# Attention ahead of an MLP on one core: the matmuls of two pairs of heads grouped by kind

## The chip, the cores and the metric

The kernel runs on one core of a Trainium2 chip. The metric is the device time of one execution in microseconds: the median of the runs of one kernel on one chip. Runs of this kernel agree within about 0.3%.

## The reference

The program computes a sigmoid attention for 8 batches, 12 heads, 448 positions and a head size of 64, and feeds its result, 3584 tokens of 768 values, to a two-layer MLP (768 to 2048 to 768).

```python
scores = q @ k.T / sqrt(64) - log(448)          # per batch and head
attn = 1 / (1 + exp(-scores))
x = (attn @ v), heads side by side               # 3584 x 768
h = x @ w_in
out = (h / (1 + exp(-1.702 * h))) @ w_out        # 3584 x 768
```

The MLP weights arrive as float64 and are turned into float32 on the core. This document is about the attention; the MLP (796.5 us of the span, from 262.5 us on) is the same in both kernels.

## The kernel before

**Work.** A *pair* is two heads of one batch, which fill the 128 partitions; there are 48 pairs. A *unit* is two pairs, 2u and 2u+1; there are 24. The 448 keys of a head are cut into three chunks of 128 (`NC`) and 64 that are left over.

- `scores(n, c)` (matmuls at L577) makes the scores of one chunk of one pair: three terms by two heads, 6 matmuls, into two PSUM banks. q and k come as a rounded part and a rest, which `split_pair` makes with a cast (ACT, L442, or DVE, L443) and a subtraction (DVE, L448).
- `scores_left(n)` (L593) makes the left-over scores of both pairs of a unit at once, in the four 64x64 quarters of the array, from the unsplit `qkraw`.
- `sigmoid` (ACT, L563) reads the two banks of one such step and writes an `a` tile in SBUF; those of the left-over scores have a ring `al` of one.
- `values(n, c)` (L608) multiplies one chunk of `a` with v, into the two banks of the unit's `av`: one bank for each pair. `values_left` (L621) adds the left-over keys of both pairs and closes both banks.
- `to_x` copies the result out of PSUM (ACT, L658, or DVE, L660). x is kept by blocks of 512 tokens, and a batch has 448, so a pair's 448 columns fall into one or two blocks: one copy for each part, into `x32` tiles of 128 x 512 that several pairs of different batches fill. When a block of a pair is full, one DMA (`split_x`) writes it to `xd` in DRAM.

**Banks.** Scores, left-over scores and `av` all take their banks from four places of two banks each, q0 to q3, in turn (`two_banks`); a place is free for the next user when the sigmoid, or the copies, that read it are done.

**Order.** `Plan` lists tasks and emits each engine's instructions in one fixed order. PE takes units of work from two streams, the attention first; inside a unit it is the order of the list. A task that has `alone = False` is not looked at when the planner decides whether a unit can begin. ACT, DVE and SP take, by estimated times, the task with the smallest key of those that are ready; `plan.early` raises a task to just before another. On the chip each engine works through its own list in order, and waits on semaphores.

**Beside the attention** run the loads of q, k (`qkraw`), v (`vraw`) and of the float64 weights (`w`, 1536 KB each), and 16 decodes of weights. A decode has a sign on ACT (L487), one exponent step on ACT or DVE (L494 or L495), and six more operations on DVE (the longest at L504 and L506). All DMAs are issued by SP in one order. After the attention the MLP begins with `first_block` (matmuls into `h`, L800); its first bank is the one that the last `av` had.

Of the kernel before, what the change touches and what calls it, by code (L numbers as in the profile page):

```python
# [8 lines left out]
F32 = mybir.dt.float32  # L9
# [10 lines left out]
P = 128  # L20
T = 512
# [15 lines left out]

# [42 lines left out]
class Plan:  # L80
# [244 lines left out]
def sigmoid_attention_mlp(ctx: ExitStack, tc: tile.TileContext, qk, v, w, out):  # L325
    nc = tc.nc
# [3 lines left out]
    NP = H // 2  # L330
# [183 lines left out]
    x32, wrote, xs = {}, {}, {}  # L514
# [121 lines left out]
    def x32_places(b, p):  # L636

        for block, into, cols in places(b):
            fresh = (block, p) not in x32
            if fresh:  # L640
                x32[block, p] = buffer("x32")
                wrote[block, p] = []
            xb = x32[block, p]

            def first(xb=xb, block=block):
                if xb.tile is None:
                    make(xb, "x32", [P, T], F32, f"x32_{block}_{p}")

            yield block, xb, first, into, cols

    copies = []

    def to_x(b, p, t, ps):
        bank = (b * NP + p) % 2
        for block, xb, first, into, cols in x32_places(b, p):
            n = cols.stop - cols.start
            copies.append(on_either(
                (0.2 + 0.00075 * n, lambda xb=xb, into=into, cols=cols: nc.scalar.copy(  # L658
                    xb.tile[:, into], ps.tile[:, bank, cols])),
                (0.15 + 0.00105 * n, lambda xb=xb, into=into, cols=cols: nc.vector.tensor_copy(  # L660
                    xb.tile[:, into], ps.tile[:, bank, cols])),
                [t], [xb, ps], first,
            ))
            wrote[block, p].append(copies[-1])
        split_x(b, p)

    def split_x(b, p):

        if b:
            xb = x32[b - 1, p]  # L670
            spilled[b - 1, p] = dma(lambda: spill[b - 1][p // NJ][:, p % NJ], lambda: xb.tile, P * T * 4 / 1024,
                                    wrote[b - 1, p], [xb])

    def make_x(block, k):
        x = buffer("pair")
        n = NJ * T

        def first():
            if x.tile is None:
                make(x, "pair", [P, 2, 4, T], F32R, f"x{block}_{k}")  # L680

        t = [dma(lambda j=j: x.tile[:, 1, j].bitcast(F32), lambda j=j: spill[block][k][:, j], P * T * 4 / 1024,
                 [spilled[block, k * NJ + j]], [x], first) for j in range(NJ)]
# [8 lines left out]
    def attention():  # L692

        units, late, held_ = [], [], 0  # L700
        for n, (b, p) in enumerate(pairs):
            t_q, qkr, t_v, vr = load_pair(b, p)
            t_s, s = split_pair(b, p, t_q, qkr)
            firsts.append(t_s)
            left = scores_left(n, [first, (t_q, qkr)], held_ + 1) if n % 2 else None
            chunks = [scores(n, c, [t_s] if n else t_q[: c + 1], s, held_ + 1 + n % 2 + c) for c in range(NC)]
            run = [t for t, _, _ in chunks]
            if n % 2 == 0:
                first, chunks0, pair0 = (t_q, qkr), chunks, (b, p)
            else:  # L710

                units.append([left[0]])
                held_ += 1
                ps = two_banks(held_)
                both = [
                    [values(m, c, got[1], got[2], t_v, vr, ps) for c, got in enumerate(cs)]
                    for m, cs in ((n - 1, chunks0), (n, chunks))
                ]
                both[1].append(values_left(*left[1:], t_v, vr, ps))
                late.append(both[0])  # L720
                copied = len(copies)
                for pair in (pair0, (b, p)):
                    to_x(*pair, both[1][-1], ps)
                urgent.append(copies[copied:])
            if n > 2 and n % 2:

                plan.early += [(t, run[0]) for t in urgent[n // 2 - 1]]

            with_v = late.pop(0) if late else []
            for t in run[2:] + with_v:  # L730
# [220 lines left out]
    def triple(one, blocks_before):  # L951
# [5 lines left out]
        def x_leaf(v):  # L957
            k, n = divmod(v, 3)
            b = plan.slot()
            view = held(b, f"x{one}_{v}", XB)  # L960
            t = dma(lambda: view().rearrange("p (j t) -> p j t", j=NJ), lambda: spill[one + n][k], P * XB * 4 / 1024,
                    [spilled[one + n, k * NJ + j] for j in range(NJ)], [b])
# [340 lines left out]
```

## Time and profile before

| | |
|---|---|
| median of 3 runs (lowest, highest) | 1059.7 us (1059.66, 1063.46) |
| the profiled execution | 1060.78 us, span of its instructions 1059.0 us |
| PE busy, of the span | 1043.6 us, 99% |
| DVE busy | 843.4 us, 80% |
| ACT busy | 554.5 us, 52% |
| attention, to the first matmul of the MLP | 262.5 us |

The page gives busy times over the whole span. The attention and the MLP have different limits, so the prediction reads the attention by itself: the timeline (start, duration, engine, line, operation, and in brackets the idle time of the engine before it and what ended it), the chain of waits (the work that ended last, traced back; start, duration, what), and the waits of PE.

### The profile page before, as it was taken

The page shows a single profiled execution, that of the slowest core. Times are in us where ns is not written, and L with a number is a line of the kernel's source. Part 1 is how long each engine was busy: PE and PEld are TensorE (multiplying, and loading weights), DVE is VectorE, ACT ScalarE, POOL GpSimd, SP SyncE. Part 2 cuts the span into 40 slices and gives each one's busy share as a digit, 9 for nine tenths or more (in the row PEclk, how much of TensorE's full clock was granted, in tenths as well). Part 3 has the DMA queues.
Part 4 walks back from the last instruction along what each step waited for, and adds up shares of the span by engine and source line. Part 5 has one row for each costly group of instructions (what it writes and reads, how often), then busy time and mean ns, then how long its engine had stood idle before and what let it go on. Part 6 is the DMA issues. An engine that isn't in the chain of part 4 may idle for free.

```text
span 1059.0 us, 13676 instructions
## 1 busy us (share of the span) xinstructions
PE 1043.6 (99%) x5300; PEld 777.5 (73%) x5300; DVE 843.4 (80%) x770; ACT 554.5 (52%) x543; POOL 0.2 (0%) x4
## 2 busy tenths in 40 slices
PE   8999999999999999999999999999999999999997
PEld 4454545454788888888888788888888888788886
DVE  5988788873999856788898989999884596888684
ACT  7888788885655523434544444332443263534342
POOL 0000000000000000000000000000000000000000
PEclk9999999999999999999999999999999999999999
DMA  9899999883799997657656665869775545445765
GB/s 353 305 334 382 337 352 324 303 318 123 299 383 401 355 388 258 238 187 236 226 169 211 224 206 181 285 214 354 275 243 191 196 139 189 148 151 150 233 199 192
DMA packets 109104, 271.44 MB, mean 256 GB/s; under 512 B 8560, under 2 KB 69104, under 8 KB 106992
## 3 DMA queue, kind: packets, MB, share of 16 engines
q1 hardware_dynamic: 109040, 270.57, 73.1%
q8 instruction: 42, 0.69, 0.2%
q14 instruction: 22, 0.18, 0.1%
HBM read 185.60 MB, written 84.93 MB: 255 GB/s over the span
## 4 chain that ended last, share of the span: by engine, by line
PE 89%; DVE 4%; DMA 3%; ACT 2%; issue 1%; SPq 0%; ACTq 0%; DVEq 0%
PE p L800 54%; PE av L608 11%; PE sc L577 9%; PE h L800 6%; PE o_q L800 6%; PE av L621 2%; PE sc L593 2%; DMA qkraw<-qk 1%; DMA w<-c 1%; DMA w<-f 1%; DMA c<-wc 1%; DVE gp L1026 1%; ACT gp L1014 1%; DVE h L743 0%; ACT o L1156 0%
## 5 line engine op out<-in xcount | busy, mean ns | idle before, releaser
L800 PE MATMUL p<-gp,w 128*128 128x512 f32 x1440 | 329.5, 390 | 2.8 <-DVE gp L1026 1.2
L800 PE MATMUL p<-xp,w 128*128 128x512 f32 x1440 | 327.9, 389 | 1.0 <-DVE xp L1026 1.0
L800 PEld LDWEIGHTS p<-gp,w 128*128 128x128 f32 x1440 | 269.7, 188 | 61.3 <-DVE gp L1026 2.0
L800 PEld LDWEIGHTS p<-xp,w 128*128 128x128 f32 x1440 | 270.2, 188 | 57.5 <-DVE xp L1026 1.4
L563 ACT ACTIVATE a<-sc,bias 128x896 f32<-128x896 f32 x168 | 158.5, 1019 | 14.9 <-PE sc L577 10.9
L608 PE MATMUL av<-a,vraw 128*64 128x448 f32 x576 | 118.6, 547 | 0.0
L577 PEld LDWEIGHTS sc<-qk 64*128 64x128 f32 x846 | 75.8, 184 | 40.8 <-issue 14.0
L577 PE MATMUL sc<-qk 64*128 64x448 f32 x846 | 98.4, 373 | 2.6 <-DVE qk L448 2.0
L608 PEld LDWEIGHTS av<-a,vraw 128*64 128x64 f32 x576 | 37.1, 136 | 59.6 <-issue 56.4
L1026 DVE TENSOR_TENSOR gp<-h,gp 128x2048 fp32r<-128x2048 f32 x31 | 70.9, 2288 | 9.3 <-ACT gp L1014 8.9
L1156 ACT COPY h<-p 128x2048 f32<-128x2048 f32 x18 | 33.7, 1875 | 82.6 <-PE p L800 53.2
L800 PE MATMUL h<-x,w 128*128 128x512 f32 x288 | 66.6, 390 | 1.3 <-DVE x L660 1.3
L800 PE MATMUL o_q<-g,w 128*128 128x512 f32 x288 | 66.6, 389 | 1.2 <-ACT graw L856 1.2
L1190 DVE TENSOR_TENSOR h<-h,p 128x2048 f32<-128x2048 f32 x23 | 52.1, 2284 | 18.6 <-PE p L800 11.4
L1014 ACT CAST gp<-h 128x2048 fp32r<-128x2048 f32 x23 | 44.0, 1912 | 43.5 <-PE p L800 36.2
L800 PEld LDWEIGHTS h<-x,w 128*128 128x128 f32 x288 | 54.0, 188 | 13.3 <-DVE x L660 2.1
L800 PEld LDWEIGHTS o_q<-g,w 128*128 128x128 f32 x288 | 54.0, 188 | 12.8 <-ACT graw L856 1.6
L1156 ACT COPY o<-p 128x1536 f32<-128x1536 f32 x18 | 25.9, 1443 | 59.3 <-PE p L800 19.2
L448 DVE TENSOR_TENSOR qk<-qkraw,qk 128x896 fp32r<-128x896 f32 x47 | 51.2, 1089 | 6.4 <-ACT qk L442 5.9
L743 DVE TENSOR_TENSOR h<-h,h 128x2048 f32<-128x2048 f32 x24 | 54.7, 2285 | 0.1
L763 ACT CAST wc<-ws 128x384 fp32r<-128x384 f32 (+1 forms) x57 | 32.2, 580 | 42.2 <-DVE ws L743 26.8
L1014 ACT CAST xp<-x 128x1536 fp32r<-128x1536 f32 x19 | 28.1, 1480 | 39.4 <-PE p L800 32.3
(107 smaller groups left out, 975.0 us busy)
## 6 DMA issues: line engine op xcount, KB each, us to landing
w<-c SPq DMA_DIRECT2D x140, 384.0 KB, 4.4
w<-c SPq DMA_DIRECT2D x52, 768.0 KB, 4.6
w<-w SPq DMA_DIRECT2D x16, 1536.0 KB, 10.0
c<-wc SPq DMA_DIRECT2D x56, 384.0 KB, 5.4
qkraw<-qk SPq DMA_DIRECT2D x47, 448.0 KB, 6.5
vraw<-v SPq DMA_DIRECT2D x24, 448.0 KB, 4.9
xd<-x SPq DMA_DIRECT2D x42, 256.0 KB, 4.6
c<-wc SPq DMA_DIRECT2D x14, 768.0 KB, 7.2
```

The source lines that it names most:

```text
L448: lambda: nc.vector.tensor_tensor(lo(), src(), hi().bitcast(F32), op=ALU.subtract),
L563: nc.scalar.activation(a.tile, ps.tile[:, :, :S], AF.Sigmoid, bias=bias, scale=scale)
L577: nc.tensor.matmul(ps.tile[:, j, :S], lhsT=src[kk][rows, S + c * P : S + (c + 1) * P], rhs=src[qq][rows, :S], start=i == 0, stop=i == len( ...
L593: nc.tensor.matmul(ps.tile[cols, j, :S], lhsT=src.tile[rows, S + NC * P :], rhs=src.tile[rows, :S], start=True, stop=True, skip_group_chec ...
L608: nc.tensor.matmul(ps.tile[cols, n % 2, :S], lhsT=vr.tile[:, at : at + D], rhs=a.tile[:, j], start=c == 0, stop=False, skip_group_check=True,)
L743: return task("DVE", cost, lambda: nc.vector.tensor_tensor(out(), x(), y(), op=op), deps, uses)
L763: t_hi = on_either((act(n), lambda: nc.scalar.copy(into()[:, 0], node.view())), (cast(n), lambda: nc.vector.tensor_copy(into()[:, 0], node ...
L800: nc.tensor.matmul(ps, lhsT=ws[:, a, c * P : (c + 1) * P], rhs=x[:, d, k], start=start and i == 0 and j == 0, stop=stop and i == len(todo) ...
L1014: t_hi = on_either((act(n), lambda: nc.scalar.copy(part(0)(), node.view())), (cast(n), lambda: nc.vector.tensor_copy(part(0)(), node.view())),
L1026: nc.vector.tensor_tensor(part(1)(), node.view(), part(0)().bitcast(F32), op=ALU.subtract)
L1156: t = on_either((act(self.n), lambda: nc.scalar.copy(view(), node.view())), (dve(self.n), lambda: nc.vector.tensor_copy(view(), node.view())),
L1190: nc.vector.tensor_tensor(view(), x.view(), y.view(), op=ALU.add if s0 == s else ALU.subtract)
```

## The change

PE's list of one unit is now: scores of pair 2u, scores of pair 2u+1, left-over scores of both, products with v of both pairs, left-over products. Only the first step of a unit (`LEADERS`) decides whether it can begin. The eight steps of a unit take the four bank places twice round; before, places were counted so that a unit advanced by one place.

`to_x` copies both banks of `av` in one instruction (128 x 896, ACT or DVE) into an `x32` tile that belongs to the unit alone, and writes each part of it to `xd` with its own DMA: 64 to 448 columns of one or two pairs. There are three such tiles (eight of the smaller ones before), and seven `a` tiles (five before).

```diff
-    qk=2, vraw=3, a=5, al=1, raw64=2, e=4, qkraw=5, x32=8,
+    qk=2, vraw=3, a=7, al=1, raw64=2, e=4, qkraw=5, x32=3,
...
+LEADERS = 1
...
+    def to_x(b, p, t, ps):
+
+        xb = buffer("x32")
+
+        def rows():
+            make(xb, "x32", [P, 2, S], F32, f"x32_{b}_{p}")
+
+        c = on_either((0.97, lambda: nc.scalar.copy(xb.tile, ps.tile[:, :, :S])),
+                      (1.09, lambda: nc.vector.tensor_copy(xb.tile, ps.tile[:, :, :S])), [t], [xb, ps], rows)
+        copies.append(c)
         for block, into, cols in places(b):
...
+            for js in ([slice(0, 2)] if p % NJ < NJ - 1 else [slice(0, 1), slice(1, 2)]):
+                k, j = divmod(p + js.start, NJ)
+                n = js.stop - js.start
+                d = dma(lambda block=block, into=into, k=k, j=j, n=n: spill[block][k][:, j : j + n, into],
+                        lambda cols=cols, js=js: xb.tile[:, js, cols], n * P * (cols.stop - cols.start) * 4 / 1024, [c], [xb])
...
-            left = scores_left(n, [first, (t_q, qkr)], held_ + 1) if n % 2 else None
-            chunks = [scores(n, c, [t_s] if n else t_q[: c + 1], s, held_ + 1 + n % 2 + c) for c in range(NC)]
-            run = [t for t, _, _ in chunks]
+            if n % 2:
+                left = scores_left(n, [first, (t_q, qkr)], held_ + 7)
+            chunks = [scores(n, c, [t_s] if n else t_q[: c + 1], s, held_ + 1 + n % 2 * NC + c) for c in range(NC)]
...
+            held_ += 8
+            ps = two_banks(held_)
+            both = [values(m, c, got[1], got[2], t_v, vr, ps)
+                    for m, cs in ((n - 1, chunks0), (n, chunks)) for c, got in enumerate(cs)]
+            both.append(values_left(*left[1:], t_v, vr, ps))
+            copied = len(copies)
+            to_x(*pair0, both[-1], ps)
+            run = [t for t, _, _ in chunks0 + chunks]
+            plan.early += [(t, run[1]) for t in urgent]
+            urgent[:] = copies[copied:]
+            unit = [*run, left[0], *both]
+            for t in unit[LEADERS:]:
                 t.alone = False
-            units.append(run + with_v)
-            if n % 2:
-                late.append(both[1])
-        units.append(late.pop())
+            units.append(unit)
```

In the lists of instructions below, `sc_0` to `sc_2` are the chunks of scores, `sc_3` the left-over scores, `av` the products with v (`a_3` is the left-over part), and a number behind `qk` or `qkraw` is the pair within its batch.

PE in the middle of the attention, before, from the left-over scores of a unit on (its left-over products follow the last row):

```order
L593 MATMUL sc_3_1553<-qkraw_0_1267 64x448 x2
L593 MATMUL sc_3_1553<-qkraw_1_1370 64x448 x2
L577 MATMUL sc_0_1567<-qk_1_1503 128x448 x6
L577 MATMUL sc_1_1577<-qk_1_1503 128x448 x6
L577 MATMUL sc_2_1591<-qk_1_1503 128x448 x6
L608 MATMUL av_1598<-a_0_1532,vraw_0_1346 64x448 x2
L608 MATMUL av_1598<-a_1_1538,vraw_0_1346 64x448 x2
L608 MATMUL av_1598<-a_2_1545,vraw_0_1346 64x448 x2
L577 MATMUL sc_0_1616<-qk_2_1536 128x448 x6
L577 MATMUL sc_1_1626<-qk_2_1536 128x448 x6
L577 MATMUL sc_2_1633<-qk_2_1536 128x448 x6
L608 MATMUL av_1598<-a_0_1587,vraw_0_1346 64x448 x2
```

and now, from the scores of a unit's second pair to the end of the unit (the scores of its first pair stand ahead of the first row):

```order
L578 MATMUL sc_0_1526<-qk_1_1453 128x448 x6
L578 MATMUL sc_1_1535<-qk_1_1453 128x448 x6
L578 MATMUL sc_2_1545<-qk_1_1453 128x448 x6
L594 MATMUL sc_3_1554<-qkraw_0_1256 64x448 x2
L594 MATMUL sc_3_1554<-qkraw_1_1360 64x448 x2
L609 MATMUL av_1562<-a_0_1512,vraw_0_1296 64x448 x2
L609 MATMUL av_1562<-a_1_1524,vraw_0_1296 64x448 x2
L609 MATMUL av_1562<-a_2_1543,vraw_0_1296 64x448 x2
L609 MATMUL av_1562<-a_0_1552,vraw_0_1296 64x448 x2
L609 MATMUL av_1562<-a_1_1560,vraw_0_1296 64x448 x2
L609 MATMUL av_1562<-a_2_1571,vraw_0_1296 64x448 x2
L622 MATMUL av_1562<-a_3_1579,vraw_0_1296 64x448 x4
```

Before, half a unit of other matmuls stood between the scores of a pair and their products; now the products of the first pair come after the scores of the second and the left-over scores, and those of the second pair directly after the first's.

ACT, between the sigmoids of two units, before:

```order
L563 ACTIVATE a_3_1252<-sc_3_1231,bias 128x896
L563 ACTIVATE a_0_1265<-sc_0_1245,bias 128x896
L563 ACTIVATE a_1_1279<-sc_1_1255,bias 128x896
L563 ACTIVATE a_2_1286<-sc_2_1269,bias 128x896
L487 ACTIVATE sign_1298<-w_15_1216 128x1536
L563 ACTIVATE a_0_1320<-sc_0_1291,bias 128x896
L563 ACTIVATE a_1_1326<-sc_1_1302,bias 128x896
L563 ACTIVATE a_2_1330<-sc_2_1309,bias 128x896
L658 COPY x_2_0_1012<-av_1276 128x192
L658 COPY x_2_1_1022<-av_1276 128x192
L563 ACTIVATE a_3_1352<-sc_3_1341,bias 128x896
```

and now:

```order
L488 ACTIVATE sign_1170<-w_14_1057 128x1536
L495 ACTIVATE expo_1157<-expo_1157 128x1536
L564 ACTIVATE a_0_1200<-sc_0_1182,bias 128x896
L564 ACTIVATE a_1_1212<-sc_1_1193,bias 128x896
L564 ACTIVATE a_2_1231<-sc_2_1203,bias 128x896
L564 ACTIVATE a_0_1240<-sc_0_1214,bias 128x896
L564 ACTIVATE a_1_1249<-sc_1_1223,bias 128x896
L564 ACTIVATE a_2_1260<-sc_2_1233,bias 128x896
L564 ACTIVATE a_3_1267<-sc_3_1242,bias 128x896
L488 ACTIVATE sign_1273<-w_15_1159 128x1536
L646 COPY x_3_0_1287<-av_1251 128x896
L564 ACTIVATE a_0_1306<-sc_0_1289,bias 128x896
```

The seven sigmoids of a unit now stand in one row, and everything else that ACT does stands between the seventh and the first of the next unit. Over the whole attention ACT has 12 of the 24 copies, 6 casts of q and k (16 before) and 9 exponent steps (2 before); DVE has the other 12 copies, 41 casts (31 before) and 7 fewer exponent steps. SP issues 56 DMAs to `xd` (42 before).

At the start of the program, ACT now:

```order
L443 CAST qk_1_242<-qkraw_1_226 128x896
L564 ACTIVATE a_0_251<-sc_0_236,bias 128x896
L564 ACTIVATE a_1_254<-sc_1_239,bias 128x896
L564 ACTIVATE a_2_265<-sc_2_246,bias 128x896
L564 ACTIVATE a_0_283<-sc_0_258,bias 128x896
L564 ACTIVATE a_1_290<-sc_1_267,bias 128x896
L564 ACTIVATE a_2_295<-sc_2_276,bias 128x896
L564 ACTIVATE a_3_299<-sc_3_285,bias 128x896
L488 ACTIVATE sign_308<-w_8_230 128x1536
```

The cast of the second pair (`qk_1`) was DVE's before and stands on ACT now, ahead of the first sigmoid. Behind the attention the lists of all four engines are the same in both kernels.

More of the change, by code (lines that the diff above doesn't have):

```diff
@@ L634, in places @@
             yield b, slice(0, S - cut), slice(cut, S)
[L636 to L649, printed above, removed]
     copies = []
     def to_x(b, p, t, ps):
[L654 to L672, printed above, removed]
+        xb = buffer("x32")
[4 more added lines that the diff above has]
+        copies.append(c)
+        for block, into, cols in places(b):
+            for js in ([slice(0, 2)] if p % NJ < NJ - 1 else [slice(0, 1), slice(1, 2)]):
[3 more added lines that the diff above has]
+                        lambda cols=cols, js=js: xb.tile[:, js, cols], n * P * (cols.stop - cols.start) * 4 / 1024, [c], [xb])
+                for i in range(n):
+                    spilled.setdefault((block, p + js.start + i), []).append(d)
     def make_x(block, k):
@@ L682, in make_x @@
         t = [dma(lambda j=j: x.tile[:, 1, j].bitcast(F32), lambda j=j: spill[block][k][:, j], P * T * 4 / 1024,
-                 [spilled[block, k * NJ + j]], [x], first) for j in range(NJ)]
+                 spilled[block, k * NJ + j], [x], first) for j in range(NJ)]
         xs[block, k] = (round_and_rest(
@@ L692, in attention @@
     def attention():
-        units, late, held_ = [], [], 0
+        units, held_ = [], 0
         for n, (b, p) in enumerate(pairs):
@@ L704, in attention @@
             firsts.append(t_s)
-            left = scores_left(n, [first, (t_q, qkr)], held_ + 1) if n % 2 else None
-            chunks = [scores(n, c, [t_s] if n else t_q[: c + 1], s, held_ + 1 + n % 2 + c) for c in range(NC)]
-            run = [t for t, _, _ in chunks]
+            if n % 2:
+                left = scores_left(n, [first, (t_q, qkr)], held_ + 7)
+            chunks = [scores(n, c, [t_s] if n else t_q[: c + 1], s, held_ + 1 + n % 2 * NC + c) for c in range(NC)]
             if n % 2 == 0:
                 first, chunks0, pair0 = (t_q, qkr), chunks, (b, p)
[L710 to L730, printed above, removed]
+                continue
+            held_ += 8
[10 more added lines that the diff above has]
+            for t in unit[LEADERS:]:
                 t.alone = False
-            units.append(run + with_v)
-            if n % 2:
-                late.append(both[1])
-        units.append(late.pop())
+            units.append(unit)
         place_of["next"] = held_ + 1
```

4 lines of the change are left out of this document (2 added, 2 removed).

## The prediction

> **What bounds the kernel now.** First the page's busy times, then the waits of PE in the attention and up to the first matmul of the MLP (what waited, for what: us in total, times, longest):
>
> ```profile
> PE 1043.6 (99%) x5300; PEld 777.5 (73%) x5300; DVE 843.4 (80%) x770; ACT 554.5 (52%) x543; POOL 0.2 (0%) x4
> ```
>
> ```profile
> PE sc L577 <- DVE qk L448: 2.0, 1, 2.0
> PE h L800 <- DVE x L660: 1.3, 1, 1.3
> PE sc L577 <- ACT x L658: 0.6, 1, 0.6
> ```
>
> PE sets the time, and in 262 us it waits 3.9 us. So the attention can only gain where PE's own stream gets shorter or one of these three waits goes, and it loses whatever new wait PE meets. The lists of all engines behind the attention are unchanged, so I take the MLP's 796.5 us as they are. PE's rows of one period, from the timeline:
>
> ```profile
> 106.39 2.09 PE L577 MATMUL sc<-qk 64*128 64x448 f32 x18
> 108.41 2.48 PE L608 MATMUL av<-a,vraw 128*64 128x448 f32 x12
> 110.81 2.09 PE L577 MATMUL sc<-qk 64*128 64x448 f32 x18
> 112.83 2.48 PE L608 MATMUL av<-a,vraw 128*64 128x448 f32 x12
> 115.24 0.98 PE L621 MATMUL av<-a,vraw 64*64 64x448 f32 x8
> 116.04 0.93 PE L593 MATMUL sc<-qkraw 64*64 64x448 f32 x8
> 116.91 2.09 PE L577 MATMUL sc<-qk 64*128 64x448 f32 x18
> ```
>
> Start to start, a pair's scores take 2.02, its products 2.41, the left-over products 0.80, the left-over scores 0.87; a unit is 116.91 - 106.39 = 10.52 us, with no gap.
>
> **Part 1, fewer changes of kind.** Here are pieces of the chain of waits in which a phase is seen in part or doubled (start, duration, what):
>
> ```profile
> 89.85 1.01 PE sc L577 x10
> ...
> 255.61 4.66 PE av L608 x24
> ```
>
> The last ten matmuls of a scores phase took 1.01 us, 0.101 each. Eighteen more inside a phase cost 1.82, where a phase of their own costs 2.02: merging two saves 0.20. The last unit has both pairs' products in one phase already: 4.66 instead of 2 x 2.41, which saves 0.16. So the two changes of kind that disappear from a unit (products to scores, scores to products) were worth 0.36, 0.18 each. But the left-over scores move. Before, they ran right after the left-over products, on the same 64x64 quarters; now they stand between scores (64x128) and products (128x64). That makes one change more. No row shows it. It lies between nothing and the 0.36 of a whole round trip; I take 0.18, the mean of the two that the rows price. Net 0.18 a unit: a period of 10.34. The products are already merged in the last unit, so there 0.20 is gained and 0.18 paid; units 1 to 22 count: 22 x 0.18 = **-4.0 us** (between 0 and -7.9).
>
> The Trainium skill ("TensorEngine Tiling (Array Packing)", Tiling Modes, Key Properties) says that changing the tiling mode drains the array, and a change of tile alone doesn't. By that the new change isn't free, five modes a unit become four, and the sum stays -4.0; without it the rows alone would allow -7.9. The trace agrees as far as it goes: a changed kind costs 0.18 in both rows that show it.
>
> **Part 2, the start.** Rows of the first 21 us:
>
> ```profile
> 6.48 0.63 DVE L443 CAST qk<-qkraw 128x896 fp32r<-128x896 f32 x1 [5.48 <-DMA qkraw<-qk]
> 7.81 0.98 PE L593 MATMUL sc<-qkraw 64*64 64x448 f32 x8
> 13.01 0.94 ACT L442 CAST qk<-qkraw 128x896 fp32r<-128x896 f32 x1 [0.17 <-DMA qkraw<-qk]
> 15.21 2.09 PE L577 MATMUL sc<-qk 64*128 64x448 f32 x18 [2.00 <-DVE qk L448]
> 20.45 0.93 PE L593 MATMUL sc<-qkraw 64*64 64x448 f32 x8
> ```
>
> Before, PE reached the scores of the third pair at 13.2 and waited 2.0 for q and k, which landed at 13.0. Now unit 0 is finished first. Its second pair's split starts at 6.48, on ACT with 0.95 and DVE with 1.09, so PE begins those scores at 8.6. The first pair's three sigmoids stand behind that cast on ACT, 1.02 for the first and 0.90 for each more (rows below): they end at 8.4, 9.3, 10.2. The scores run to 10.6, the left-over scores to 11.5; the fourth sigmoid ends at 11.1 and frees the bank of the products, which run to 16.1 (4.63), the left-over ones to 17.0. The third pair is long ready by then (13.0 + 0.63 + 1.09 = 14.7). Before, the same work was done at 20.45 - 2.02 = 18.4, since by 20.45 the third pair's scores were made as well. **-1.4 us** (between 0 and the 2.0 of the wait).
>
> **Part 3, the copies.** First by groups (count, then total and mean ns, then idle time before), then the last ones on the timeline:
>
> ```profile
> L658 ACT COPY x<-av 128x448 f32<-128x448 f32 x4 | 2.1, 533 | 3.1 <-PE av L621 2.0 <-DVE x L660 1.1
> L658 ACT COPY x<-av 128x128 f32<-128x128 f32 x5 | 1.3, 266 | 6.0 <-DVE x L660 4.9 <-PE av L621 1.1
> L660 DVE COPY x<-av 128x448 f32<-128x448 f32 x4 | 2.5, 624 | 1.7 <-ACT x L658 1.7
> ```
>
> ```profile
> 261.25 0.53 ACT L658 COPY x<-av 128x448 f32<-128x448 f32 x1 [3.62 <-PE av L621]
> 261.82 0.62 DVE L660 COPY x<-av 128x448 f32<-128x448 f32 x1 [7.72 <-ACT x L658]
> 262.50 16.66 PE L800 MATMUL h<-x,w 128*128 128x512 f32 x72 [1.31 <-DVE x L660]
> ```
>
> ACT: 0.83 ns a column and 0.16, so 0.91 for 896 columns; DVE about twice 0.62 less a start, 1.1. The copies of a unit ran one after the other; now there is one. At the end PE waits 1.0 instead of 1.3: **-0.3**. The wait of 0.6 at 96.4 came from such a row of copies: **-0.6** (between 0 and -0.6). Elsewhere a copy is hidden: the first chunk of the next unit doesn't need its bank. The fourth does, 1.9 us into the unit, and a copy on DVE that starts when `av` is ready, 0.15 into it, is done at 1.3. That leaves 0.6 for an operation that DVE has under way; the longest is 1.75 (below), so at worst a copy is 1.15 late, and PE with it.
>
> **Part 4, the new wait.** Rows of ACT beside PE:
>
> ```profile
> 116.29 0.32 ACT L658 COPY x<-av 128x192 f32<-128x192 f32 x1 [1.16 <-PE av L621]
> 117.32 3.71 ACT L563 ACTIVATE a<-sc,bias 128x896 f32<-128x896 f32 x4
> 121.33 1.88 PE L577 MATMUL sc<-qk 64*128 64x448 f32 x16
> 122.30 1.01 ACT L563 ACTIVATE a<-sc,bias 128x896 f32<-128x896 f32 x1 [1.27 <-PE sc L577]
> ```
>
> A sigmoid can start 0.97 after its phase's first matmul (121.33 to 122.30), lasts 1.02, and each further one adds (3.71 - 1.02)/3 = 0.90. With a unit's first score at 0 they end at 2.0, 2.9, 3.8, 4.7, 5.6, 6.5, 7.4. PE's fifth and sixth chunks reuse the first two places at 2.5 and 3.1: 0.5 and 0.2 to spare. The left-over scores come at 3.84 and need the place of the third, free at 3.8; the products come at 4.71 and need that of the fourth, free at 4.7. So PE and ACT meet there with **nothing to spare**, where before half a unit (4.4 us) lay between. An ACT copy ahead doesn't hurt: it starts 1.05 after the left-over products (115.24 to 116.29), 0.15 into the unit, and is done at 1.0. I charge 0.05 a unit for hand-overs, 23 x 0.05 = **+1.2** (between 0 and the rival's +13.0 below).
>
> What else ACT does must fit between 7.4 and the next unit's 10.34 + 0.97 = 11.3, so into 3.9. Groups of the attention, the loads of weights (count, KB, us to landing), and SP's longest wait:
>
> ```profile
> L487 ACT ACTIVATE sign<-w 128x1536 bf16<-128x1536 int16 x16 | 26.1, 1634 | 0.0
> L442 ACT CAST qk<-qkraw 128x896 fp32r<-128x896 f32 x16 | 15.1, 947 | 0.2 <-DMA qkraw<-qk 0.2
> L494 ACT ACTIVATE expo<-expo 128x1536 uint16<-128x1536 uint16 x2 | 3.0, 1496 | 0.0
> L448 DVE TENSOR_TENSOR qk<-qkraw,qk 128x896 fp32r<-128x896 f32 x47 | 51.2, 1089 | 6.4 <-ACT qk L442 5.9
> L495 DVE TENSOR_SCALAR expo<-expo 128x1536 uint16<-128x1536 uint16 x14 | 7.8, 557 | 0.0
> L506 DVE SCALAR_TENSOR_TENSOR w<-w,expo 128x1536 f32<-128x1536 f32 x16 | 28.1, 1754 | 0.2
> ```
>
> ```profile
> w<-w SPq DMA_DIRECT2D x16, 1536.0 KB, 10.0
> ```
>
> ```profile
> SPq L416 <- PE av L621: 97.0, 19, 7.7
> ```
>
> The fullest gaps of the new order hold a sign, an exponent step and a copy: 1.63 + 1.50 + 0.91 = 4.0, less 0.1 where instructions overlap. They just fit. DVE changes by +10 casts of 0.62, -7 exponent steps of 0.56 and less copying, about zero in sum; the splits that the next unit needs have 8 us from the chunk that frees their buffer. The loads of weights are issued when the left-over scores free `qkraw`, 4.7 into a unit, land 10.0 later, 4.4 into the next, and ACT asks at 7.4. The 14 more DMAs to `xd` cost SP no time that counts: its queue stands 97 us waiting for a buffer of v, and the copy that refills an `x32` tile comes three units later.
>
> **Sum.** -4.0 - 1.4 - 0.3 - 0.6 + 1.2 = -5.1. The profiled execution took 1060.78 with a span of 1059.0; span and time fall alike, to 1053.9 and 1055.7. The median of the runs is 1059.7, 1.1 below the profiled one: **1054.6 us**.
>
> **Rivals.**
> 1. ACT becomes the pacemaker. For it: nothing is spared at the two meeting points, and a late first sigmoid passes to PE one to one. Sixteen units carry a sign. If it comes half its length late in each (0.82 us), PE loses 13.0 in place of the 1.2: -6.3 + 13.0 = +6.7, **1066.4**. It decides from 6.3/23 = 0.27 us a unit on. Against it: 3 us between landing and use, and gaps that fit. Chance 0.10. The Trainium skill ("TensorEngine Tiling (Array Packing)", Performance Considerations, PSUM Bottleneck) warns of this: tiling speeds TensorE up but not the emptying of PSUM. Here the trace has 6.4 us of sigmoids beside 10.3 of PE, so ACT is late at one place at most, not in sum.
> 2. The new change of kind costs the whole 0.36: part 1 is worth nothing, -1.4 - 0.9 + 1.2 = -1.1, **1058.6**. For it: 64x64 beside 128x64 on both sides was never seen without its neighbour. Chance 0.15.
> 3. It is free, and PE meets no wait: -7.9 - 1.4 - 0.9 = -10.2, **1049.5**. Chance 0.10.
> 4. The change doesn't do what it says: the new lists show the phases merged, so only the planner's estimates could make the chip's waits differ widely. Chance 0.03, no change, 1059.7.
>
> **How the numbers follow.** The forecast has 0.62, with 1051.5 to 1058 as its own range (each unit 0.13 better or 0.15 worse). About 0.5%, 5.3 us, is what can be told from no change; the edge is at 1054.4, inside the forecast. Faster: 0.31 of it and rival 3, with 0.03 of rival 2: 0.44. Slower (over 1065.0): 0.08 of rival 1. Same: the rest, 0.48. The range, 1050.5 to 1061, leaves out most of rivals 1 and 3.
>
> **What would show it.** PE's period of 10.3 to 10.4 with four phases, of which scores last 3.84 and products 4.6; the first scores of unit 1 near 17.0; the last wait ahead of `h` at 1.0; PE waits for ACT of some tenths at `sc_3` and the first product. Wrong: waits of PE for ACT or DVE of more than 6 us in sum, a period over 10.5, or a first matmul of the MLP after 262.5; and MLP times that differ by more than 1 us.

## The result, and the profile after

The changed kernel takes **1053.47 us** (median of 4 runs, 1053.04 to 1054.89) beside 1060.85 for the kernel before on the same chip (4 runs, 1059.66 to 1063.46): a ratio of 0.993, with a 95% interval of 0.9917 to 0.9943. That is faster by 0.7%, and the whole interval lies beyond the 0.5% that can be told from no change. The forecast was 1054.6 with a range of 1050.5 to 1061; the time lies in it, 1.1 us below the forecast. The forecast started from a median before of 1059.7 (three runs); with the fourth run it is 1060.85. So the forecast drop of 5.1 us stands beside a measured one of 7.4: part of the closeness of the two times is luck. Of the three cases, "faster" (by more than 0.5%) had been given 0.44 and "same" 0.48.

The profiled execution took 1053.04 us, with a span of 1051.2 (before: 1060.78 and 1059.0). The page's busy times after:

```profile
PE 1038.1 (99%) x5300; PEld 778.9 (74%) x5300; DVE 841.9 (80%) x741; ACT 552.7 (53%) x512; POOL 0.2 (0%) x4
```

PE has the same 5300 matmuls and is busy 5.5 us less; DVE and ACT are busy about as long as before. So the change did not take work away: it shortened PE's stream. The waits of PE up to the first matmul of the MLP (besides one in the program's first two microseconds, which both kernels have):

```profile
PE h L773 <- ACT x L646: 1.0, 1, 1.0
PE sc L578 <- DVE qk L449: 0.9, 1, 0.9
```

The wait for the third pair, 2.0 before, is gone; a new one of 0.9 for the second pair stands at the start, as the forecast's 8.6 for those scores had it. The wait for a copy in the middle, 0.6, is gone. No wait for a sigmoid came in. The chain of waits shows a unit (start, duration, what):

```profile
16.73 3.83 PE sc L578 x36
20.56 0.91 PE sc L594 x8
21.47 4.66 PE av L609 x24
26.13 0.91 PE av L622 x8
27.04 3.84 PE sc L578 x36
```

The chain is PE alone, and the next row begins where the last one ends. The period is 27.04 - 16.73 = 10.31 here and 10.33 in the other units (10.51 before). Of it, scores take 3.84 instead of 2 x 2.02, products 4.66 instead of 2 x 2.41; the two left-over steps take 0.91 each instead of 0.87 and 0.80. So merging gave 0.20 + 0.16, and the new place of the left-over scores cost 0.15. (Starts in the chain lie up to 0.1 behind those of the timeline; differences within one view agree.)

The start and the end of the attention, from the timeline of ACT and PE (start, duration, in brackets the idle time before and what ended it; the window cuts the second and the last row of PE short):

```profile
5.94 0.94 ACT L443 CAST qk<-qkraw 128x896 fp32r<-128x896 f32 x1 [3.72 <-DMA qkraw<-qk]
```

```profile
8.15 2.09 PE L578 MATMUL sc<-qk 64*128 64x448 f32 x18 [0.90 <-DVE qk L449]
16.66 3.71 PE L578 MATMUL sc<-qk 64*128 64x448 f32 x34
...
255.25 7.12 PE L773 MATMUL h<-x,w 128*128 128x512 f32 x30 [1.03 <-ACT x L646]
```

The first scores of unit 1 come at 16.66 (18.43 before for the same work), and the MLP begins at 255.25 instead of 262.50: **7.25 us earlier**. From there to the end of the span it takes 796.0, 0.5 less than before.

### The profile page after: what moved, and what is told of

Same layout as the page of the kernel before. It is cut to its first block, busy times and chain, and to the rows that moved or that the text cites. A ratio compares the mean times of both kernels' runs of the same rounds, so it can differ in the third digit from the quotient of the medians.

```text
span 1051.2 us, 13595 instructions
## 1 busy us (share of the span) xinstructions
PE 1038.1 (99%) x5300; PEld 778.9 (74%) x5300; DVE 841.9 (80%) x741; ACT 552.7 (53%) x512; POOL 0.2 (0%) x4
## 4 chain that ended last, share of the span: by engine, by line
PE 91%; DVE 3%; DMA 3%; ACT 2%; issue 1%; SPq 0%; ACTq 0%; DVEq 0%
PE p L773 55%; PE av L609 11%; PE sc L578 9%; PE h L773 6%; PE o_q L773 6%; PE av L622 2%; PE sc L594 2%; DMA c<-wc 1%; ACT gp L987 1%; DVE o L1130 1%; SPq L417 0%; DVE gp L999 0%; DVE gs L716 0%; ACT o L1129 0%; DMA qkraw<-qk 0%
## 5 line engine op out<-in xcount | busy, mean ns | idle before, releaser
L564 ACT ACTIVATE a<-sc,bias 128x896 f32<-128x896 f32 x168 | 153.6, 1025 | 17.9 <-PE sc L578 17.9
L609 PE MATMUL av<-a,vraw 128*64 128x448 f32 x576 | 113.5, 543 | 0.0
L578 PE MATMUL sc<-qk 64*128 64x448 f32 x846 | 92.0, 368 | 0.9 <-DVE qk L449 0.9
L1163 DVE TENSOR_TENSOR h<-h,p 128x2048 f32<-128x2048 f32 x23 | 52.1, 2284 | 17.6 <-PE p L773 10.4
```

Source lines behind the costliest of these rows:

```text
L564: nc.scalar.activation(a.tile, ps.tile[:, :, :S], AF.Sigmoid, bias=bias, scale=scale)
L578: nc.tensor.matmul(ps.tile[:, j, :S], lhsT=src[kk][rows, S + c * P : S + (c + 1) * P], rhs=src[qq][rows, :S], start=i == 0, stop=i == len( ...
L609: nc.tensor.matmul(ps.tile[cols, n % 2, :S], lhsT=vr.tile[:, at : at + D], rhs=a.tile[:, j], start=c == 0, stop=False, skip_group_check=True,)
L1163: nc.vector.tensor_tensor(view(), x.view(), y.view(), op=ALU.add if s0 == s else ALU.subtract)
```

## The experiments

Eleven more runs were made, one of them (e7) of the changed kernel again. The table has the median of each, its ratio to the kernel before on the same chip, and the first matmul of the MLP in its trace. The period is the usual one, start to start of a unit. The edits are against the changed kernel unless another is named, and show the lines that matter; `...` marks what is left out.

| kernel | median, us | ratio (95% interval) | MLP begins | period |
|---|---|---|---|---|
| the change | 1053.47 | 0.993 (0.9917 to 0.9943) | 255.25 | 10.33 |
| e1, left-over scores first | 1054.39 | 0.9938 (0.9922 to 0.9953) | 255.59 | 10.30 |
| e2, left-over scores between | 1057.42 | 0.9961 (0.9947 to 0.9975) | 259.27 | 10.52 |
| e3, copies alone | 1060.5 | 0.9994 (0.9985 to 1.0004) | 262.35 | 10.51 |
| e4, order alone | 1062.44 | 1.001 (1.0001 to 1.002) | 263.90 | 10.3 to 10.97 |
| e5, ACT late by 0.6 | 1066.81 | 1.0059 (1.0038 to 1.0081) | 267.58 | 10.88 |
| e6, five `a` tiles | 1054.27 | 0.9939 (0.9921 to 0.9957) | 256.09 | 10.33 |
| e7, the change again | 1053.93 | 0.9939 (0.992 to 0.9958) | 255.57 | 10.33 |
| e8, e1 with a shorter sigmoid | 1055.21 | 0.9941 (0.9927 to 0.9955) | 257.53 | 10.17 |
| e9, the change with it | 1054.27 | 0.9933 (0.9918 to 0.9948) | 255.54 | 10.33 |
| e10, left-over scores a unit ahead | 1052.04 | 0.9914 (0.9898 to 0.993) | 253.76 | 10.17, 10.30 |
| e11, e10 with copies on DVE | 1052.84 | 0.9923 (0.9908 to 0.9939) | 252.82 | 10.17 |

The theory was the prediction's: a change of kind on PE costs about 0.18 us, and the number of them sets the period as long as ACT and the copies keep up. The rivals: the gain comes from the copies or from the two more `a` tiles; or ACT is already what sets the pace.

### One change of kind more, one less

In e2 the left-over scores stand between the scores of the two pairs: five changes of kind a unit instead of four.

```diff
...
-            unit = [*run, left[0], *both]
+            unit = [*run[:NC], left[0], *run[NC:], *both]
```

The bank places are counted along with the new order, here and in e1.

> The changed kernel with the left-over scores moved between the scores of the two pairs: five changes of kind in a unit instead of four, and no sigmoid later than before. Theory A: period 10.33 + 0.18 = 10.51, span 1051.2 + 23 x 0.18 = 1055.3. Theory B (scores of a unit in two runs, products in one): the scores lose the 0.20 that their merging gave, the same 1055 to 1056; this run therefore tells A and B apart only together with the one that has the left-over scores first. If a wait for ACT is what limits, more than 1057.

One unit of its chain of waits:

```profile
100.44 2.02 PE sc L578 x18
102.46 0.91 PE sc L594 x8
103.38 2.01 PE sc L578 x18
105.39 4.66 PE av L609 x24
110.05 0.91 PE av L622 x8
110.96 2.02 PE sc L578 x18
```

The period is 110.96 - 100.44 = 10.52: 0.19 more than with four changes, and the same as before the change, which also has five. The scores alone account for it: 2.02 + 2.01 - 3.84 = 0.19. By itself this run can't tell the number of changes from the length of the runs of scores, since it alters both; the next one leaves the runs of scores and products whole.

In e1 the left-over scores come first in the unit, right behind the left-over products of the unit before: three changes.

```diff
...
-            unit = [*run, left[0], *both]
+            unit = [left[0], *run, *both]
```

> The changed kernel with the left-over scores moved to the front of each unit, where they follow the left-over products of the unit before, on the same 64x64 quarters: three changes of kind in a unit instead of four. Theory A (the time is the sum of PE's phases, and each change of kind costs about 0.18 us): period 10.15 instead of 10.33 us, 23 x 0.18 = 4.1 us less, first matmul of the MLP near 251.1, span near 1047. Theory B (the gain of the change came from the longer runs of scores and products, not from the number of changes of kind): period 10.33, span 1051 as in the changed kernel. Rival on ACT: the sigmoid of the left-over scores now comes first, and if ACT has no time there PE waits and the period is over 10.33.

A unit of its chain of waits:

```profile
100.04 0.75 PE sc L594 x8
100.80 3.87 PE sc L578 x36
104.67 0.04 issue
104.71 4.73 PE av L609 x24
...
110.35 0.75 PE sc L594 x8
```

The left-over scores now take 0.75 instead of 0.91, so the change of kind was saved: 0.16. But the period is only 110.35 - 100.04 = 10.31. The rest went back at the products, which start late (the row "issue") and run 0.07 longer. ACT shows why:

```profile
100.95 6.40 ACT L564 ACTIVATE a<-sc,bias 128x896 f32<-128x896 f32 x7 [1.52 <-PE sc L594]
```

On the timeline the left-over scores of this unit begin at 99.86, so the first sigmoid begins 1.09 into the unit. The fourth one frees the bank of the products at 1.09 + 1.02 + 3 x 0.90 = 4.81, and the products, which could come at 4.70, come at 104.71 - 99.86 = 4.85. One unit of this trace took 11.05, with a wait of 0.6 for a copy on DVE; that is most of why the MLP begins no earlier than in the changed kernel.

To test that reading, e8 is e1 with the sigmoid of the left-over scores shortened to one of its two banks, and e9 does the same to the changed kernel, where that sigmoid is the last of its row. Both leave out the sigmoid of every second head's left-over keys, so they compute something else; PE's work is the same. The edit that both have:

```diff
-            nc.scalar.activation(a.tile, ps.tile[:, :, :S], AF.Sigmoid, bias=bias, scale=scale)
+            js = slice(0, 1 if tag == "al" else 2)
+            nc.scalar.activation(a.tile[:, js], ps.tile[:, js, :S], AF.Sigmoid, bias=bias, scale=scale)
...
-                        ps.tile[cols, k, :S], lhsT=vr.tile[rows, at : at + D], rhs=a.tile[rows, j],
+                        ps.tile[cols, k, :S], lhsT=vr.tile[rows, at : at + D], rhs=a.tile[rows, 0],
```

> The order with the left-over scores first in the unit, and the sigmoid of the left-over scores cut to one of its two banks (448 columns, about 0.53 us on ACT instead of 0.90); both left-over products read that bank, so the sigmoid of every second head's left-over keys is left out. PE's work is as in the run with the left-over scores first. Theory (a change of kind costs about 0.2, and that run kept only a part of it because its fourth sigmoid ended at 4.79, after the left-over scores and chunks had ended at 4.62): the fourth sigmoid now ends at about 4.4, the products start at about 4.62 to 4.70 without a wait, the period is 10.15 to 10.2, and the first matmul of the MLP comes at 252 to 253 instead of 255.6; the median is about 1051. Rival (ACT was not what held that run; the saved change of kind is given back on PE itself): the period stays at 10.3 and the first matmul of the MLP at 255.5.

> The changed kernel with the sigmoid of the left-over scores cut to one of its two banks, as in the run beside it, and nothing else. Theory (the changed kernel never waits for ACT, and this sigmoid is the seventh of its row, ahead of 3 us in which ACT has other work): nothing changes, the period stays 10.33, the first matmul of the MLP at 255.2 and the median at 1053.5, within 0.5. Rival (ACT still costs the changed kernel something that the rows don't show, such as a late first sigmoid behind a sign): relieving ACT of 0.37 us a unit gains 1 to 3 us.

The first and the next unit's first row, from the chain of waits of e8:

```profile
103.70 0.75 PE sc L595 x8
...
113.87 0.75 PE sc L595 x8
```

The period is 113.87 - 103.70 = 10.17 in 18 of 22 units, without a gap, as the theory had it; in e9 it stays at 10.33 in all units but one (10.71). So ACT was what held e1, and it costs the changed kernel nothing. The runs of scores and products are those of the changed kernel, so the 0.16 that e8 saves comes from the change of kind and not from longer runs. The time of e8 was missed, though: 1055.2 where 1051 was expected. Three units took 10.47, 11.59 and 14.11, 5.7 us more than three of 10.17 (a fourth took 10.23), and most of that began with a late copy on DVE. The row of PE's waits, two of DVE's timeline, and the row of PE behind the longer wait:

```profile
PE sc L579 <- DVE x L648: 3.3, 2, 2.1
```

```profile
78.08 0.96 DVE L444 CAST x<-x 128x1536 fp32r<-128x1536 f32 x1 [2.18 <-DMA x<-xd]
...
82.50 1.08 DVE L648 COPY x<-av 128x896 f32<-128x896 f32 x1
```

```profile
83.64 4.26 PE L579 MATMUL sc<-qk 64*128 64x448 f32 x24 [2.10 <-DVE x L648]
```

DVE's list has a cast for the MLP in it, and DVE stood 2.18 us waiting for its data from DRAM. The copy of `av` came behind it, and began 3.3 after its unit (which began at 79.19); PE waited 2.1 for it, the longer of its two waits. The 24 matmuls behind that wait then took 4.26, where 2.70 were usual: the granted clock was 0.50 from 84 to 86 us.

### Each half of the change alone

e3 is the kernel before with the new copies: one instruction for both banks, tiles of a unit, a DMA for each part. PE's order is the old one.

The edit is against the kernel before; the new `to_x` is that of the changed kernel.

```diff
-    qk=2, vraw=3, a=5, al=1, raw64=2, e=4, qkraw=5, x32=8,
+    qk=2, vraw=3, a=5, al=1, raw64=2, e=4, qkraw=5, x32=3,
...
-                for pair in (pair0, (b, p)):
-                    to_x(*pair, both[1][-1], ps)
+                to_x(*pair0, both[1][-1], ps)
```

> The kernel before with the new copies alone: one copy of 128x896 for each unit into three tiles, and the 56 smaller writes to memory; the order of the matmuls is that of before. If the copies are hidden except at two places: 0.3 us less at the end of the attention and the 0.6 us wait at 96 us gone, a span of 1058.1 (1057.5 to 1059.0). If the copies themselves are what was gained: 1051 to 1054.

The waits for copies went as expected: 1.0 at the end, and none in the middle. On the timelines of PE, the kernel before first, then e3:

```profile
94.00 0.93 PE L593 MATMUL sc<-qkraw 64*64 64x448 f32 x8
...
105.53 0.93 PE L593 MATMUL sc<-qkraw 64*64 64x448 f32 x8
```

```profile
95.20 0.93 PE L593 MATMUL sc<-qkraw 64*64 64x448 f32 x8
...
105.71 0.93 PE L593 MATMUL sc<-qkraw 64*64 64x448 f32 x8
```

That unit took 11.53 before and takes 10.51 here: the wait shown as 0.6 cost 1.0. With the 0.3 at the end that is 1.3 gained; still the MLP begins only 0.15 earlier, since unit 1's left-over scores came 1.2 later in this execution (21.62 instead of 20.45). The stretch from 16 to 20 us (span, busy time of PE, PEld, DVE, ACT and POOL, granted clock, DMA share, GB/s), the kernel before first, then e3:

```profile
16.00:20.00 4.00, 4.00 (x30) 1.90 (x30) 4.00 (x5) 3.78 (x5) 0.00 (x0) 1.00 0.98 403
16.00:20.00 4.00, 4.00 (x20) 1.68 (x18) 3.97 (x5) 2.56 (x3) 0.00 (x0) 0.57 0.99 403
```

The granted clock was 0.57 there, right behind the 2.0 us in which PE waits for the third pair; in the kernel before, the same wait left it at 1.00. The first products behind it took 3.65 instead of 2.48. This is one execution; by the medians, the copies alone can't be told from no change, and even without that loss they would give 1.3 of the 7.25.

e4 has the new order with the old copies (and five `a` tiles).

```diff
...
-            to_x(*pair0, both[-1], ps)
+            for pair in (pair0, (b, p)):
+                to_x(*pair, both[-1], ps)
...
```

> The new order of the matmuls with the old copies (two to four small ones for each unit, one after the other on ACT and DVE, into eight tiles; five a tiles, for want of room). The old copies of a unit end about 1.7 us into the next one (they took 105.77 to 107.31 in the kernel before), where the first sigmoid should start at 0.93. Theory: they hold the sigmoids up by about 0.6, PE waits for most of it in the units with four copies (18 of 24): 18 x 0.5 = 9 us more than the changed kernel, a span near 1060, so that the order alone gains nothing. Rival: ACT takes a sigmoid between two copies or DVE takes the late ones, and PE waits for nothing: 1051 to 1053.

A unit's beginning on its timeline, PE, ACT and DVE together:

```profile
58.86 4.43 PE L578 MATMUL sc<-qk 64*128 64x448 f32 x36
...
59.37 0.55 DVE L661 COPY x<-av 128x384 f32<-128x384 f32 x1
59.95 0.59 ACT L659 COPY x<-av 128x64 f32<-128x64 f32 x2 [0.75 <-DVE x L661]
60.43 3.72 ACT L564 ACTIVATE a<-sc,bias 128x896 f32<-128x896 f32 x4
63.31 0.98 PE L594 MATMUL sc<-qkraw 64*64 64x448 f32 x8
```

The copies of a unit run by turns on ACT and DVE, and ACT's last one ends 1.7 into the unit. So the first sigmoid begins at 60.43 - 58.86 = 1.57 instead of 0.93, and the left-over scores come at 63.31 - 58.86 = 4.45 instead of 3.84. That unit is among the worst: about half of the units take 10.83 or more, and most of the others 10.4 to 10.6. The mean period is 10.70, and the order alone is 0.1% slower than before. With one copy on one engine the same order gains 7.4 us.

### How much room ACT has

e5 puts one more instruction behind the first sigmoid of every unit: ACT copies half an `a` tile onto itself.

```diff
...
+            if again:
+                nc.scalar.copy(a.tile[:, 0], a.tile[:, 0])
...
```

> The changed kernel with one more instruction on ACT in each unit, directly behind the first sigmoid: a copy of 448 columns of that a tile onto itself (about 0.43 us behind a neighbour, more where it waits for the sigmoid's write). The order of everything else is kept. In the changed kernel the third sigmoid ends 3.76 into a unit and the left-over scores, which need its bank, start at 3.84. Theory (nothing to spare): all but 0.08 of the delay passes to PE, 0.35 to 0.5 us in each of 24 units, 8 to 12 us more, a span of 1059 to 1063. Rival (ACT has room that the ends of its instructions don't show): under 2 us more, 1051 to 1053.

Rows of ACT's timeline, of PE's waits and of PE's timeline:

```profile
93.22 1.01 ACT L564 ACTIVATE a<-sc,bias 128x896 f32<-128x896 f32 x1
94.26 0.57 ACT L566 COPY a<-a 128x448 f32<-128x448 f32 x1
94.73 5.50 ACT L564 ACTIVATE a<-sc,bias 128x896 f32<-128x896 f32 x6
```

```profile
PE sc L580 <- ACT a L564: 4.2, 22, 0.2
```

```profile
92.27 3.31 PE L580 MATMUL sc<-qk 64*128 64x448 f32 x30
95.80 0.88 PE L580 MATMUL sc<-qk 64*128 64x448 f32 x6 [0.21 <-ACT a L564]
...
103.17 1.08 PE L580 MATMUL sc<-qk 64*128 64x448 f32 x8
```

The second sigmoid begins 94.73 - 93.22 = 1.51 after the first, where 0.90 was usual: 0.61 late. The unit takes 103.17 - 92.27 = 10.90 instead of 10.33, so 0.57 of the 0.61 reaches PE. The waits of PE name only 4.2 us (0.2 in each of 22 units, at the sixth chunk) of the 12.3 by which the MLP begins later. The rest lies inside phases: the six matmuls behind the listed wait take 0.89 to the next phase (it begins at 96.69), where 6 x 0.101 = 0.61 was usual. The time is above what was expected, mostly since the added delay was 0.61 and not the 0.43 that had been estimated.

e6 is the changed kernel with five `a` tiles, as before it:

```diff
-    qk=2, vraw=3, a=7, al=1, raw64=2, e=4, qkraw=5, x32=3,
+    qk=2, vraw=3, a=5, al=1, raw64=2, e=4, qkraw=5, x32=3,
```

> The changed kernel with five a tiles instead of seven. The sixth sigmoid of a unit then takes the tile of the first, which the products free at 4.75 + 0.75 = 5.5 into the unit; it would have started at 5.43. If only that counts, the sixth and seventh sigmoids come 0.1 to 0.2 later, long before their products (8.5 and 9.4): no change, 1051.2. If the rings of a tiles were part of the gain: a wait of PE at the products, over 1053.

The period stays at 10.33 in most units; six took 0.05 to 0.09 more. The two more tiles are no part of the gain that can be measured (1054.27 beside 1053.93 for the changed kernel on the same chip). The changed kernel itself, run again beside it:

> The changed kernel once more, beside the two above on the same chip: a span of 1051.2 within 0.5, a time of 1053 to 1054.

### A version that goes on from there

e1 and e8 say what is left: 0.16 a unit, if ACT does not begin its row with the left-over scores. In e10 the left-over scores of the *next* unit stand ahead of the left-over products of this one. That is three changes of kind as well, and their sigmoid runs before the unit's first scores.

```diff
-    qk=2, vraw=3, a=7, al=1, raw64=2, e=4, qkraw=5, x32=3,
+    qk=2, vraw=3, a=6, al=2, raw64=2, e=4, qkraw=5, x32=3,
...
+            at = (2, 3, here if n > 1 else 0, 1 - here if n > 1 else 1, 2, 3)
...
-            unit = [*run, left[0], *both]
+            if units:
+                plan.early.append((left[1], units[-1][-1]))
+                units[-1].insert(-1, left[0])
+            units.append([*run, *([] if units else left[:1]), *both])
...
```

> The whole computation, with the left-over scores of the next unit put between a unit's products and its left-over products: scores, products, left-over scores of the next unit, left-over products of this one. A second `al` tile and six `a` tiles; places so that the two open ones change roles from unit to unit. Theory: three changes of kind a unit, as in the run with the left-over scores first (period 10.15), and here the left-over sigmoid runs ahead of the unit's first scores, so that ACT has only six sigmoids in the row and the fourth step's ends at about 3.75, before the products come at 3.84 less 0.1. Where DVE copies, the period is 10.15 to 10.2; where ACT copies (about half the units), the copy stands between the left-over sigmoid and the first one (0.33 to 1.2 into the unit), the first sigmoid starts 0.25 late and the products 0.1 to 0.2. First matmul of the MLP at 252 to 254, the median 1050.5 to 1052.5. Rival: q and k of the next unit, which the left-over scores now want 1.6 us earlier, land too late, and PE waits for them: no better than 1053.5.

Rows of the timelines of DVE, ACT and PE:

```profile
110.24 1.09 DVE L647 COPY x<-av 128x896 f32<-128x896 f32 x1 [0.46 <-PE av L622]
```

```profile
109.52 1.01 ACT L564 ACTIVATE a<-sc,bias 128x896 f32<-128x896 f32 x1 [1.56 <-PE sc L594]
111.08 5.50 ACT L564 ACTIVATE a<-sc,bias 128x896 f32<-128x896 f32 x6 [0.56 <-PE sc L578]
...
120.59 0.90 ACT L646 COPY x<-av 128x896 f32<-128x896 f32 x1
121.38 1.02 ACT L564 ACTIVATE a<-sc,bias 128x896 f32<-128x896 f32 x1
```

```profile
110.11 3.91 PE L578 MATMUL sc<-qk 64*128 64x448 f32 x36
...
120.27 3.96 PE L578 MATMUL sc<-qk 64*128 64x448 f32 x36
...
130.58 1.71 PE L578 MATMUL sc<-qk 64*128 64x448 f32 x14
```

The unit at 110.11, whose copy is on DVE, takes 10.16. The one at 120.27 has ACT's copy between its first two sigmoids; its first scores' sigmoid begins 1.11 in instead of 0.97, and it takes 10.31. e11 is the same with all copies on DVE (the edit is against e10):

```diff
-        c = on_either((0.97, lambda: nc.scalar.copy(xb.tile, ps.tile[:, :, :S])),
-                      (1.09, lambda: nc.vector.tensor_copy(xb.tile, ps.tile[:, :, :S])), [t], [xb, ps], rows)
...
+        c = task("DVE", 1.09, copy, [t], [xb, ps])
```

> As the run beside it, with all copies of results on DVE. Theory: no unit has an ACT copy between its sigmoids, so the period is 10.15 to 10.2 throughout, the first matmul of the MLP comes at 251.5 to 252.5 (its last wait 1.2 instead of 1.0), and the median is 1049.5 to 1050.5. Rival: DVE, which gets about twelve copies more, is late with some of them (a place is wanted 1.93 into the unit and a copy in time ends at 1.23), each such unit losing 0.5 to 2 us: no better than the run beside it.

Its period is 10.17 in 21 of 22 units, and no copy makes PE wait until the last one (1.2). The MLP begins at 252.82, 2.4 us before the changed kernel's, a little later than expected; but the MLP took 797.1 here, 1.1 longer than in the changed kernel. Its median, 1052.84, missed the 1049.5 to 1050.5 that was expected and lies above e10's. The trace is of the fastest of its six runs (1051.66); three took 1053.9 to 1054.6, and no trace shows why. Both are clearly faster than the kernel before. e10 has the lowest time, 1.4 us below the changed kernel; the intervals of the two ratios overlap, so that lead shows in the traces (253.76 against 255.25) but not yet surely in the times.

## Why the prediction came out as it did

**Part 1, fewer changes of kind (-4.0): right.** The period was forecast at 10.34 and is 10.33; 22 x (10.51 - 10.33) = 4.0. The new change, for which no row existed, costs 0.15 (0.18 had been taken). The experiments make a row of it: three changes of kind a unit give 10.17 (e8, e11), four 10.33, five 10.52 (e2, and 10.51 before). Each costs 0.16 to 0.19. Rival 2 (0.36 for the new one) and the half of rival 3 that had it free are out; the other half, no wait, came true (part 4). The Trainium skill ("TensorEngine Tiling (Array Packing)", Tiling Modes, Key Properties) says that changing the tiling mode drains the array while a change of tile alone does not. The trace agrees as to the price: the left-over scores cost 0.75 behind the left-over products, on the same 64x64 tiles, and 0.91 behind scores.

**Part 2, the start (-1.4): right in kind.** Unit 1 began at 16.66 where 17.0 was forecast, so it was -1.8. The step that was off is the landing of the second pair: its cast began at 5.94, the forecast took 6.48 from the trace before. That moves from one execution to the next: in e7, the same kernel, unit 1 began at 16.97. (The products, forecast at 4.63, take 4.66.)

**Part 3, the copies (-0.3 and -0.6): the end right, the middle too small.** The last wait is 1.0, as forecast. The wait at 96.4 was priced at the 0.6 that the list of waits gives; the unit that held it was 1.0 longer than the others, and that is what went (e3).

**Part 4, the new wait (+1.2): the step that failed.** PE and ACT do meet where it said, but the price was wrong: the charge of 0.05 a unit for hand-overs was not paid at all, and the waits for ACT at `sc_3` and the first product did not come. The timelines of the changed kernel give the margin, for the unit that begins at 109.59:

```profile
110.53 6.40 ACT L564 ACTIVATE a<-sc,bias 128x896 f32<-128x896 f32 x7
```

```profile
109.59 3.91 PE L578 MATMUL sc<-qk 64*128 64x448 f32 x36
113.43 0.98 PE L594 MATMUL sc<-qkraw 64*64 64x448 f32 x8
114.34 4.73 PE L609 MATMUL av<-a,vraw 128*64 128x448 f32 x24
```

The first sigmoid begins 0.94 in, so the third ends at 0.94 + 1.02 + 2 x 0.90 = 3.76 and the fourth at 4.66. The left-over scores come at 3.84 and the products at 4.75: about 0.09 to spare at both. The forecast's own rows, unrounded, gave 0.05 and 0.02, which it called "nothing to spare"; the sigmoid began 0.03 earlier than it took, and the left-over scores ran 0.04 longer. In e1 the fourth sigmoid ended at 4.81 and the products came at 4.85, so a hand-over takes about 0.04, and about 0.05 of the 0.09 is real room (an estimate from these rows). e5 agrees with that: of its 0.61, 0.55 to 0.57 reach PE. So the room is small enough that e1 and e5 pay nearly all of their delay, and large enough that the change pays none. Rival 1 is out for this kernel: ACT's copies, signs and exponent steps did fit between the rows of sigmoids, and e9, with ACT relieved, gains nothing. Its price, a delay that passes to PE one to one, was nearly right, as e5 shows. The Trainium skill ("TensorEngine Tiling (Array Packing)", Performance Considerations, PSUM Bottleneck) warns that the copy out of PSUM may become the bottleneck. The trace of the changed kernel does not show it; in e1 and e4, where a bank is read late, it costs 0.14 a unit (10.31 beside 10.17 in e8) and 0.37 (10.70 beside 10.33).

**The sum.** Up to the MLP the forecast was -4.0 - 1.4 - 0.3 - 0.6 + 1.2 = -5.1. Measured: -4.0 - 1.8 - 0.3 - 1.0 + 0 = -7.1, and 7.25 in the trace; the rest of 0.15 I leave open. The MLP, taken as unchanged, was 0.5 shorter in this execution. The prediction leaned to "same" by 0.04, with the edge of "faster" at 1054.4; without the 1.2 that wasn't paid it would have been 1053.4, on the other side of that edge. The time came out 1.1 from the forecast, and not 2.3 as the drop did, because the median before rose by 1.15 between the two.

Neither half does it by itself (e3 1060.5, e4 1062.4, both within 0.2% of before), so the gain belongs to the pair: the order takes the changes of kind out, and the single copy keeps the row of sigmoids early enough that PE does not give the gain back.

## What to carry to other kernels

Count the changes between tile forms in PE's list, price one from two rows that differ by it, and group the matmuls by form, the small ones of one form next to each other, across units if need be. Before merging, write down for each reused bank when its reader ends and when PE comes back: here a margin of a tenth of a microsecond was enough while the reader's row began on time, and a row that began late passed nearly all of it to PE. So what stands ahead of that row on the reader's engine, and any wait for a DMA in the same list, is to be judged together with the order.

## What the runs showed of the hardware

- A change of tile form on PE cost 0.16 to 0.19 us wherever it was added or removed (3, 4 or 5 a unit), in the places that were tried. Of two steps of 64x64 tiles side by side, with other operands and another bank, the second took 0.75 where it takes 0.91 behind another form.
- Delays that come from a bank were listed as waits only in part: of the 12.3 us that e5 lost up to the MLP, 4.2 stand in the waits of PE; the wait at 96.4 in the kernel before, listed as 0.6, cost 1.0.
- In the attention of the thirteen traces the granted clock fell in two places, each behind a wait of PE of about 2 us: to 0.57 in e3 (16 to 20 us, behind 2.0) and to 0.50 in e8 (84 to 86 us, behind 2.1). The kernel before had the same wait as e3 and kept 1.00, and so did e10 behind 1.7. What decides, no run here tells.
